# Retention attention and a top-1 expert layer on one core: states by chunks, one-hot placement, gathered rows

## The chip, the core and the metric

The program runs on one NeuronCore of a Trainium2 chip. Its engines have an instruction queue each: TensorE (PE in the rows; its weight loads are PEld), VectorE (DVE), ScalarE (ACT), GpSimd (POOL) and the queue that only issues transfers (SP). Matrix products are written to PSUM and are copied from there to SBUF by DVE or ACT; GpSimd does not read PSUM. The metric is device microseconds of one execution of the whole program, lower is better.

## The reference

Inputs are q, k and v of 8 batches, 8 heads, 576 positions and 64 channels, and the weights of 8 experts (512 to 1024 to 512), all float32.

```python
scores = q @ k.T / 8                               # per batch and head
gamma  = 1 - 2.0 ** (-5 - h)                       # per head
ret    = scores * where(i >= j, gamma ** (i - j), 0)
x      = (ret @ v), heads side by side             # 4608 tokens x 512
logits = x @ w_gate                                # 8 experts
e      = argmax(logits); gate = softmax(logits)[e] # one expert for a token
out    = gate * (relu(x @ w1[e]) @ w2[e])
```

There is no softmax in the attention. Because gamma ** (i - j) is gamma ** i times gamma ** -j, the decay can be multiplied into q and k beforehand, and only the triangular mask is left.

## The kernel before

**Attention, L156 to L268.** The loops go over 8 batches and 4 pairs of heads. SP loads both heads' q, k and v (L168, and L172 for the last 64 positions), and DVE multiplies the decay into q and k (L177 to L187). TensorE turns both with products against the identity (L197, L199, L208, L210); the two heads go to the lower and the upper 64 partitions of one PSUM tile, and DVE and ACT copy it out in turn (L203, L205, L212). For each of five blocks of k, TensorE multiplies it with all q at or after it (L225, L229); DVE masks the square on the diagonal (L231), and ACT copies what is right of it (L234, L236). All of these pass through one pool of four PSUM tiles, `psW`. Then the products with v are accumulated over the five blocks (L255, L259), and ACT copies the result, turned (channels by tokens), to `xTc` (L263 to L267). All of it is float32. A float32 product is two matmul instructions for TensorE, and so is each of these in the counts of the profile: 512 columns by 64 in L255 occur 64 times for 32 pairs of heads and head A.

**Routing, L269 to L347, once a batch.** The logits are computed turned (L272, L278). For each of five blocks of tokens they are turned back (L285), and so is x (L289, with the transpose instruction), which ACT casts to bfloat16 (L292). DVE finds the expert, the gate and, with two products against a triangle and a square of ones (L310, L312) and a running `carry`, the token's row in a table of 8 times 768 rows. GpSimd scatters the row of x (L332) and the token's number and gate (L340) into two DRAM tables, `sorted_x` and `sorted_meta`, which were filled with blanks at the start (L136, L143).

**Experts, L349 to L417.** For each expert ACT issues the loads of the weights (L362, L366; 2 MB each); ACT casts w1 (L364) and DVE w2 (L368). SP loads the expert's 768 rows turned, in two transfers of 384 (L380). For each 384 columns: 8 times 4 matmuls into `psh` (L392), ACT's relu to `hT` (L394), and for each of three blocks of 128 tokens 8 matmuls into `psy` (L399). DVE casts the token's number (L404) and multiplies by the gate (L406), and GpSimd scatters 128 rows of 2 KB to `out` (L408): 48 scatters in all. The framework sees every scatter as a write to all of `out`, so each one waits until the one before has landed; GpSimd works its queue in order. The order of the instructions in each queue is made by a list scheduler from their dependences and a cost model, with the order of the program as priority.

## Time and profile before

| | |
|---|---|
| median of three runs | 818.26 us |
| the runs | 823.42, 818.26, 817.86 us |
| span of the profiled execution | 826.1 us |
| mean granted TensorE clock of the profiled execution | 0.863 of full speed |
| DMA, mean over the span | 109 GB/s, 89.66 MB in all |
| DVE, ACT and POOL, busy share | 36%, 38%, 16% |

The profiled execution is 1.0% above the median of the runs. A busy time is the union of an engine's instructions; a matmul's end is modelled and includes the time its last column needs to come out, so that a busy TensorE is not one at its peak. In the granted clock 1.0 is 2.4 GHz and 0.5 is 1.2 GHz.

### The profile page before, as it was taken

The numbers are of one execution on the slowest core, as the hardware profiler recorded it, in microseconds if no ns is written. First come the engines' busy times: TensorE is split into PE (matmuls) and PEld (weight loads), VectorE is DVE, ScalarE is ACT, GpSimd is POOL, SyncE is SP. The second block draws the span as 40 slices with busy tenths as digits, with TensorE's granted clock in tenths as the row PEclk, the third lists the DMA queues.
The fourth block names the chain that finished last, engine by engine and source line by source line (L and its number), as shares of the span: only waits on it lengthen the run. The fifth ranks groups of instructions, "written<-read, shape, count | busy, mean of one in ns | idle before, by whom it ended". The sixth has DMA issues, their size and how long they took to land. (4 is left out here: it accounts for less than half of the span.)

```text
span 826.1 us, 13290 instructions
## 1 busy us (share of the span) xinstructions
PE 677.2 (82%) x4568; PEld 412.3 (50%) x4584; DVE 297.3 (36%) x1472; ACT 316.3 (38%) x889; POOL 134.1 (16%) x141
## 2 busy tenths in 40 slices
PE   0899899799999989989989989940967678599782
PEld 0666565565655656656556556530533243254341
DVE  4354444534534434534534453322121212212321
ACT  3244354344344335335325434412433144254230
POOL 0000400300310220120030040012011312213222
PEclk9999599789789789979959978965878797899997
DMA  9532232223223133223213222085798475553221
GB/s 301 129 80 58 58 80 67 56 68 80 55 54 80 30 74 78 51 60 80 58 52 87 59 59 58 18 302 156 247 348 246 158 182 166 180 152 89 59 68 58
DMA packets 175220, 89.66 MB, mean 109 GB/s; under 512 B 153262, under 2 KB 159406, under 8 KB 175152
## 3 DMA queue, kind: packets, MB, share of 16 engines
q1 hardware_dynamic: 155568, 41.04, 22.5%
q10 hardware_dynamic: 12544, 33.56, 11.6%
q0 software_dynamic: 7040, 14.21, 4.7%
q8 instruction: 36, 0.59, 0.4%
q14 instruction: 32, 0.26, 0.1%
HBM read 61.93 MB, written 24.21 MB: 104 GB/s over the span
## 5 line engine op out<-in xcount | busy, mean ns | idle before, releaser
L225 PE MATMUL psa<-qTp,kTp 64*128 64x512 f32 (+4 forms) x640 | 168.9, 485 | 22.6 <-ACT rt L234 19.0
L225 PEld LDWEIGHTS psa<-qTp,kTp 64*128 64x128 f32 (+1 forms) x640 | 87.9, 185 | 75.5 <-ACT rt L234 53.3
L399 PE MATMUL psy<-w2b,hT 128*128 128x512 bf16 x368 | 97.3, 411 | 32.9 <-DVE ysb L406 31.4
L392 PE MATMUL psh<-xTg,w1b 128*128 128x384 bf16 x512 | 95.9, 348 | 31.5 <-ACT w1b L364 18.2
L394 ACT ACTIVATE hT<-psh 128x384 bf16<-128x384 f32 x128 | 61.6, 490 | 143.3 <-PE psh L392 106.3
L332 POOL DMA_INDIRECT sorted_x<-xb,posi x40 | 39.3, 982 | 453.9 <-DVE mx L296 232.5
L234 ACT COPY rt<-psa 128x384 f32<-128x384 f32 (+3 forms) x256 | 88.3, 361 | 58.2 <-DVE rt L231 54.0
L255 PE MATMUL psxmB<-rt,tf 128*64 128x512 f32 (+3 forms) x256 | 105.6, 514 | 0.0
L255 PE MATMUL psxmA<-rt,tf 128*64 128x512 f32 (+3 forms) x256 | 104.9, 510 | 0.0
L199 PE MATMUL pst<-ident,tf 128*64 128x128 f32 x512 | 85.1, 316 | 17.4 <-DVE tf L177 17.4
L231 DVE TENSOR_TENSOR rt<-psa,trimask 128x128 f32<-128x128 f32 (+1 forms) x320 | 79.1, 268 | 43.8 <-PE psa L225 40.7
L197 PE MATMUL pst<-ident,tf 128*64 128x128 f32 x512 | 85.0, 316 | 11.3 <-ACT qTp L205 5.2
L392 PEld LDWEIGHTS <-w1b 128*128 128x128 bf16 x512 | 52.7, 103 | 74.0 <-issue 24.4
L408 POOL DMA_INDIRECT out_dram<-ysb,tid x48 | 54.0, 1124 | 198.6 <-DVE tid L404 96.7
L399 PEld LDWEIGHTS <-hT 128*128 128x128 bf16 x384 | 39.9, 104 | 85.2 <-issue 49.0
L197 PEld LDWEIGHTS pst<-ident,tf 128*64 128x64 f32 x512 | 64.4, 157 | 20.4 <-ACT qTp L205 11.0
L199 PEld LDWEIGHTS pst<-ident,tf 128*64 128x64 f32 x512 | 64.4, 157 | 17.8 <-DVE tf L177 17.8
L404 DVE CAST tid<-meta 128x1 int32<-128x1 f32 x48 | 7.4, 153 | 173.0 <-DMA out_dram<-ysb,tid 140.8
L259 PEld LDWEIGHTS psxqA<-rt,tf 128*64 128x64 f32 x256 | 38.4, 154 | 37.3 <-issue 28.5
L263 ACT COPY xTc<-psxmA 64x512 f32<-64x512 f32 x32 | 18.5, 578 | 97.4 <-PE psxmA L255 49.1
L203 DVE COPY qTp<-pst 128x128 f32<-128x128 f32 x64 | 18.6, 291 | 81.1 <-PE pst L199 61.9
L292 ACT CAST xb<-psx 128x512 bf16<-128x512 f32 (+1 forms) x40 | 23.4, 584 | 59.9 <-PE psx L289 43.4
(97 smaller groups left out, 927.4 us busy)
## 6 DMA issues: line engine op xcount, KB each, us to landing
w1f<-in_moe_w_dram ACTq DMA_DIRECT2D x8, 2048.0 KB, 8.1
w2f<-in_moe_w_dram ACTq DMA_DIRECT2D x8, 2048.0 KB, 9.5
tf<-in_q_dram SPq DMA_DIRECT2D x64, 128.0 KB, 2.4
tf<-in_k_dram SPq DMA_DIRECT2D x64, 128.0 KB, 2.4
tf<-in_v_dram SPq DMA_DIRECT2D x64, 128.0 KB, 2.4
sorted_x<-zin SPq DMA_DIRECT2D x1, 6144.0 KB, 20.3
tt<-in_q_dram SPq DMA_DIRECT2D x64, 16.0 KB, 2.2
tt<-in_k_dram SPq DMA_DIRECT2D x64, 16.0 KB, 2.2
```

What stands on the lines that cost most here:

```text
L197: nc.tensor.matmul(out=pst[0:Dh, 0:P], lhsT=tfA[:, c, :], rhs=ident[:, :], start=True, stop=True)
L199: nc.tensor.matmul(out=pst[Dh:2 * Dh, 0:P], lhsT=tfB[:, c, :], rhs=ident[:, :], start=True, stop=True)
L225: nc.tensor.matmul(out=psa[0:ni, 0:nA], lhsT=kTp[half:half + 64, c0:c0 + ni], rhs=qTp[half:half + 64, c0:c0 + nA], start=True, stop=True)
L231: nc.vector.tensor_tensor(out=rt[0:ni, 0:ni], in0=psa[0:ni, 0:ni], in1=trimask[0:ni, 0:ni], op=ALU.mult)
L234: nc.scalar.copy(out=rt[0:ni, ni:nA], in_=psa[0:ni, ni:nA])
L255: nc.tensor.matmul(out=psm[half:half + 64, c0:SM], lhsT=lhsV, rhs=rt[0:ni, 0:SM - c0], start=(i == 0), stop=last_main)
L259: nc.tensor.matmul(out=psq_[half:half + 64, 0:SQ], lhsT=lhsV, rhs=rt[0:ni, SM - c0:S - c0], start=(i == 0), stop=(i == nqb - 1))
L332: nc.gpsimd.indirect_dma_start(out=sorted_x[:, :], out_offset=bass.IndirectOffsetOnAxis(ap=posi[:, 0:1], axis=0), in_=xb16[:, :], in_offse ...
L392: nc.tensor.matmul(out=psh[0:P, 0:GT], lhsT=w1b[:, c, fb * P:(fb + 1) * P], rhs=xTg[:, c, :], start=(c == 0), stop=(c == NDC - 1))
L394: nc.scalar.activation(out=hT[:, fb, :], in_=psh[0:P, 0:GT], func=AF.Relu)
L399: nc.tensor.matmul(out=psy[0:P, 0:Dm], lhsT=hT[:, fc, blk * P:(blk + 1) * P], rhs=w2b[:, fc, :], start=(fc == 0), stop=(fc == NFB - 1))
L408: nc.gpsimd.indirect_dma_start(out=out[:, :], out_offset=bass.IndirectOffsetOnAxis(ap=tid[:, 0:1], axis=0), in_=ysb[:, :], in_offset=None, ...
```

## The change

The kernel is written anew; the shapes are constants.

- **Attention by chunks.** The work goes in 40 units, 5 for a batch: 4 pairs of heads over 512 positions in 4 chunks of 128, and one unit for the last 64 positions of all 8 heads. GpSimd multiplies the decay into k and q (`kk`, `qq`, in `stage_T`), and TensorE turns them with the transpose instruction. A state for each pair of heads, k times v summed over the chunks up to each, is accumulated in PSUM (`stage_S`) and copied by ACT into block-diagonal tiles `sall`. Scores are computed within a chunk only (`stage_SC`); one DVE instruction per head masks all four chunks. `stage_AV` adds scores times v and, for the chunks after the first, q times the state of the chunks before. `stage_XR` multiplies the result with a matrix that is the identity beside the gate's weights, so that x by rows and the pair's share of the logits come out of one product; ACT casts x to bfloat16, and SP stores it to `x_rows` in DRAM, in token order.
- **Order.** Every TensorE instruction is pinned to program order: scores of unit i, rows of unit i - 1, transposes and state of unit i + 1, then the values of unit i. Each PSUM tile has a name and one buffer of its own.
- **Routing in two halves** of 2304 tokens, 20 columns of 128: after batch 3 (during units of batches 4 and 5), and at the end of the attention. The expert, the gate and the token's rank are found for all 20 columns at once; `place` builds one-hot matrices of slots (`rh`, 128 by 128 per column) and a payload per column, and 20 (then 40) matmuls put the tokens' numbers and gates into the slots of all experts.
- **Experts in two passes**: 256 slots per expert from the first half and 384 for the rest, 5 blocks of 128 per expert and 40 in all. A block's rows are fetched from `x_rows` by an indirect gather (`gather`, GpSimd) and turned by TensorE (`trans`). Weights come in pieces of 512 KB on SP's queue; those of two experts are loaded during the attention and cast by GpSimd, the others four pieces a step with casts in turn on ACT, DVE and GpSimd. The scatter to `out` is as before, with the slots' numbers made beforehand and four buffers.
- **A general path** behind a branch at the end runs all tokens that found no slot, if an expert's second pass would need more than 384.
- The blank-filled tables, their zeroing, the transposing loads and the scatters of x and of the numbers are gone.

The added code, cut to its core (the removed code stands above):

```diff
+NT = B * NCOL
+GT = NT // 2
+CA = 256
+CB = 384
...
+    def pin(i):
+        tc.keep_in_program_order(i)
+        return i
+    def mm(out, lhsT, rhs, start, stop):
+        return pin(nc.tensor.matmul(out=out, lhsT=lhsT, rhs=rhs, start=start, stop=stop,
+                                    skip_group_check=True))
...
+        def kv(dst, src, hs):
+            if hs is None:
+                for c in range(NCH):
+                    nc.sync.dma_start(out=dst[:, c, :, :],
+                                      in_=src[b, :, c * P:(c + 1) * P, :].rearrange("h p d -> p h d"))
+            else:
+                for h in range(hs.start, hs.stop):
+                    nc.sync.dma_start(out=dst[:, :, h, :],
+                                      in_=src[b, h, 0:NCH * P, :].rearrange("(c p) d -> p c d", p=P))
...
+    loads = {0: load_batch(0, 4)}
...
+    casts = [nc.gpsimd.tensor_copy, nc.scalar.copy, nc.vector.tensor_copy]
+    def load_w(e, part, eng):
...
+        st = stpool.tile([P, F], F32, tag="st", name="wst")
+        c = part % 4
+        if part < 4:
+            nc.sync.dma_start(out=st[:, :], in_=moe_w1[e, c * P:(c + 1) * P, :])
+            casts[eng](out=w1b[:, c, :, :, :].rearrange("p j s m -> p j m s"),
+                       in_=st[:, :].rearrange("p (j m s) -> p j m s", m=P, s=2))
...
+    def stage_T(u):
+        b, p = u
+        qt, kt, vt, qk, vr = loads[b]
+        if p < NP:
+            h0 = 2 * p
+            kk = wkp.tile([P, NCH, P], F32, tag="kk")
+            nc.gpsimd.tensor_tensor(
+                out=kk[:, :, :].rearrange("p c (h d) -> p c h d", d=DH), in0=kt[:, :, h0:h0 + 2, :],
+                in1=kg[:, 0:NCH, h0:h0 + 2].unsqueeze(3).to_broadcast([P, NCH, 2, DH]), op=ALU.mult)
+            qq = wkp.tile([P, NCH, P], F32, tag="qq")
...
+            psq = ps1.tile([P, 4 * P], F32, tag="Q")
+            for s in range(4):
+                pin(nc.tensor.transpose(out=psq[:, s:4 * P:4], in_=qq[:, s, :], identity=ident[:, :]))
+            psk = ps1.tile([P, 4 * P], F32, tag="K")
+            for c in range(NCH):
+                pin(nc.tensor.transpose(out=psk[:, c * P:(c + 1) * P], in_=kk[:, c, :], identity=ident[:, :]))
+            qT = wkp.tile([P, 4 * P], F32, tag="qT")
+            nc.vector.tensor_copy(out=qT[:, :], in_=psq[:, :])
+            kT = wkp.tile([P, 4 * P], F32, tag="kT")
+            nc.scalar.copy(out=kT[:, :], in_=psk[:, :])
+            st_[u] = dict(kk=kk, qT=qT, kT=kT)
...
+        pss = ps1.tile([P, NCH, DH], F32, tag="S")
+        for c in range(NCH):
+            n = NCH - c
+            for j in range(2):
+                mm(pss[j * DH:(j + 1) * DH, c:NCH, :], kk[:, c, j * DH:(j + 1) * DH],
+                   vt[:, c, 2 * p + j, :].unsqueeze(1).to_broadcast([P, n, DH]), c == 0, c == NCH - 1)
+        sa = sall[b % 2]
+        nc.scalar.copy(out=sa[0:DH, p, :, 0:DH], in_=pss[0:DH, :, :])
+        nc.scalar.copy(out=sa[DH:P, p, :, DH:P], in_=pss[DH:P, :, :])
...
+            for c in range(NCH):
+                for ps, r in ((psa, slice(0, DH)), (psb, slice(DH, P))):
+                    mm(ps[:, c, :], kT[r, c * P:(c + 1) * P], qT[r, c * P:(c + 1) * P], True, True)
...
+            nc.vector.tensor_tensor(out=sa[:, :, :], in0=psa[:, :, :], in1=m, op=ALU.mult)
+            nc.vector.tensor_tensor(out=sb[:, :, :], in0=psb[:, :, :], in1=m, op=ALU.mult)
...
+            psx = ps1.tile([P, NCH, P], F32, tag="XT")
+            for c in range(NCH):
+                for j in range(2):
+                    mm(psx[j * DH:(j + 1) * DH, c, :], vt[:, c, 2 * p + j, :], d["sc"][j][:, c, :], c == 0, False)
+            for c in range(1, NCH):
+                mm(psx[:, c, :], sl[:, p, c - 1, :], qT[:, c * P:(c + 1) * P], False, c == NCH - 1)
+            xT = wkp.tile([P, NCH, P], F32, tag="xT")
+            nc.scalar.copy(out=xT[:, :, :], in_=psx[:, :, :])
...
+        psr = ps1.tile([P, 2, 512], F32, tag="XR")
+        n = P if p < NP else REM
+        for c in range(4):
+            mm(psr[0:n, c // 2, (c % 2) * IWN:(c % 2 + 1) * IWN], xT[:, c, :],
+               iw[:, p if p < NP else c, :], True, True)
...
+            nc.scalar.copy(out=xr[:, 0:NCH, p * P:(p + 1) * P].rearrange("p (a c) f -> p a c f", c=2),
+                           in_=r[:, :, :, 0:P])
+                nc.vector.tensor_tensor(out=l, in0=r[:, :, :, P:IWN], in1=l, op=ALU.add)
+                nc.sync.dma_start(out=x_rows[b * S:b * S + NCH * P, :].rearrange("(c p) d -> p c d", p=P),
+                                  in_=xr[:, 0:NCH, :])
...
+        mm(psr[:, 0:n], su1[:, :], oh[:, g, :, :].rearrange("p e t -> p (e t)"), True, False)
+        mm(psr[:, n:n + E], onesb[:, :], incl[:, :, GT - 1], False, False)
+        mm(psr[:, 0:n], onesb[:, :], incl[:, :, :].rearrange("p e t -> p (e t)"), False, True)
...
+    def place(ph, pool, psp):
+        nb = (CA if ph == 0 else CB) // P
+        nt = GT if ph == 0 else NT
+        w = E * nb
...
+        for f in range(NFLD):
+            eng = nc.vector if f % 2 == 0 else nc.gpsimd
+            eng.tensor_tensor(out=pay[:, :, f, :], in0=ohb[:, :, :, :].rearrange("p t b e -> p t (b e)"),
+                              in1=fld[:, 0:nt, f].unsqueeze(2).to_broadcast([P, nt, w]), op=ALU.mult)
+        rh = pool.tile([P, nt, P], BF16, tag=f"rh{ph}")
+        for t in range(nt):
+            nc.vector.tensor_scalar(out=rh[:, t, :], in0=iota_r[:, :], scalar1=r[:, t:t + 1], scalar2=None,
+                                    op0=ALU.is_equal)
+        for t in range(nt):
+            mm(psp[:, 0:NFLD * w], rh[:, t, :], pay[:, t, :, :].rearrange("p f w -> p (f w)"), t == 0, t == nt - 1)
...
+    def gather(e, ph):
+        nb = (CA if ph == 0 else CB) // P
+        nr = NTOK // 2 if ph == 0 else NTOK
+        for j in range(nb):
+            i = j * E + e
+            xg = gp.tile([P, DM], BF16, tag="xg", name="xg")
             nc.gpsimd.indirect_dma_start(
+                out=xg[:, :], out_offset=None, in_=x_rows[0:nr, :],
+                in_offset=bass.IndirectOffsetOnAxis(ap=slots[ph][1][:, i:i + 1], axis=0),
+                bounds_check=nr - 1, oob_is_err=False)
+            gat_t[(e, ph, j)] = xg
...
+    stage_T(units[0])
+    stage_S(units[0])
+    for i, u in enumerate(units):
+        b, p = u
+        if p == 0 and b + 1 < B:
+            loads[b + 1] = load_batch(b + 1, 1)
+        stage_SC(u)
+        if i > 0:
+            stage_XR(units[i - 1])
+        if i + 1 < len(units):
+            stage_T(units[i + 1])
+        if i + 1 < len(units):
+            stage_S(units[i + 1])
+        stage_AV(u)
+        for (e, pt) in w_at.get(i, []):
+            load_w(e, pt, 0)
+        if u == (B // 2, 1):
+            incl0 = softmax_top1(0, rtmp)
+        if u == (B // 2, 2):
+            ps = ps1.tile([P, 512], F32, tag="Q")
+            ranks(0, incl0, rtmp, ps)
+        if u == (B // 2 + 1, 0):
+            ps = ps1.tile([P, 512], F32, tag="Q")
+            place(0, rtmp, ps)
+        if u == (B - 2, 0):
+            gather(0, 0)
+            gather(1, 0)
+    stage_XR(units[-1])
...
+    seq = [(0, 0), (1, 0), (0, 1), (1, 1)] + [(e, ph) for e in range(2, E) for ph in (0, 1)]
...
+            for c in range(NPT):
+                pin(nc.tensor.transpose(out=pt[:, c, :], in_=xg[:, c * P:(c + 1) * P], identity=identb[:, :]))
+            nc.vector.tensor_copy(out=xt[:, :, j * P:(j + 1) * P], in_=pt[:, :, :])
...
+        per = 2 if ph == 0 else 1
+        for f0 in range(0, NFB, per):
+            pm = psH.tile([P, per, n], F32, tag="ph")
+            for o in range(per):
+                fb = f0 + o
+                for c in range(NPT):
+                    mm(pm[:, o, :], w1b[:, c, fb // 2, fb % 2, :], xt[:, c, :], c == 0, c == NPT - 1)
+            nc.scalar.activation(out=ht[:, f0:f0 + per, :], in_=pm[:, :, :], func=AF.Relu)
...
+            py = psY.tile([P, DM], F32, tag="py")
             for fb in range(NFB):
+                mm(py[:, :], ht[:, fb, j * P:(j + 1) * P], w2b[:, fb // 2, fb % 2, :], fb == 0, fb == NFB - 1)
+            ys = yp.tile([P, DM], F32, tag="ys")
+            nc.vector.tensor_scalar(out=ys[:, :], in0=py[:, :], scalar1=gat[:, i:i + 1], scalar2=None, op0=ALU.mult)
+            nc.gpsimd.indirect_dma_start(
+                out=out[:, :], out_offset=bass.IndirectOffsetOnAxis(ap=tids[:, i:i + 1], axis=0),
+                in_=ys[:, :], in_offset=None, bounds_check=NTOK - 1, oob_is_err=False)
...
+            load_w(e, pt, (1, 2, 0)[nq[0] % 3])
...
+    trans(0, 0)
+    more_w(4)
+    incl1 = softmax_top1(1, rtm2)
+    for i, (e, ph) in enumerate(seq):
+        ht = mm1(e, ph)
+        if i == 0:
+            ps = psT.tile([P, 512], F32, tag="pt", name="psrk")
+            ranks(1, incl1, rtm2, ps)
+        if i + 1 < len(seq):
+            trans(*seq[i + 1])
+        mm2(e, ph, ht)
+        if i == 0:
+            ps = psT.tile([P, 512], F32, tag="pt", name="pspl")
+            place(1, rtm2, ps)
+        if i + 2 < len(seq):
+            gather(*seq[i + 2])
+        more_w(4)
...
+    over = nc.values_load(fi[0:1, 0:1], min_val=0, max_val=NTOK,
+                          skip_runtime_bounds_check_because="a count of tokens")
+    with tc.If(over > 0):
...
```

## Rows read from the trace of the kernel before

**Rows 1.** The page: busy times; granted clock in tenths, in 40 slices.

```profile
PE 677.2 (82%) x4568; PEld 412.3 (50%) x4584; DVE 297.3 (36%) x1472; ACT 316.3 (38%) x889; POOL 134.1 (16%) x141
...
PEclk9999599789789789979959978965878797899997
```

**Rows 2.** Stretches: start:end, length, busy time by engine, clock, DMA share.

```profile
...
0.00:22.00 22.00, 1.94 (x8) 1.56 (x8) 8.31 (x61) 7.93 (x33) 1.75 (x13) 1.00 0.93 299
22.00:546.00 524.00, 485.51 (x3672) 316.89 (x3672) 228.20 (x1275) 217.11 (x716) 70.64 (x72) 0.88 0.28 69
546.00:592.00 46.00, 16.20 (x73) 8.41 (x74) 9.31 (x39) 12.79 (x15) 7.90 (x9) 0.60 0.66 213
592.00:746.00 154.00, 116.94 (x535) 57.03 (x544) 31.78 (x61) 55.33 (x84) 31.48 (x28) 0.84 0.69 206
746.00:826.00 80.00, 56.63 (x284) 28.45 (x287) 19.75 (x38) 23.10 (x41) 22.36 (x20) 0.91 0.24 67
```

**Rows 3.** The chain that ended last: shares, then pieces (start, us).

```profile
DMA out_dram<-ysb,tid 17%; POOLq L408 0%; POOLq L442 0%
...
643.94 2.68 DMA out_dram<-ysb,tid
656.14 5.80 DMA out_dram<-ysb,tid
```

**Rows 4.** The scatters to `out`; GpSimd's last two (start, us).

```profile
L408 POOL DMA_INDIRECT out_dram<-ysb,tid x48: 966/971/2468, 591.9 to 822.2; - x48
...
818.84 0.97 POOL L408 DMA_INDIRECT out_dram<-ysb,tid  x1 [2.48 <-DMA out_dram<-ysb,tid]
822.18 0.97 POOL L408 DMA_INDIRECT out_dram<-ysb,tid  x1 [2.37 <-DMA out_dram<-ysb,tid]
```

**Rows 5.** TensorE in order of time, one head pair (start, us).

```profile
306.79 1.53 PE L225 MATMUL psa<-qTp,kTp 64*128 64x512 f32 x4
...
311.14 1.41 PE L225 MATMUL psa<-qTp,kTp 64*128 64x192 f32 x8 [0.78 <-ACT rt L234]
312.48 0.64 PE L255 MATMUL psxmA<-rt,tf 128*64 128x512 f32 x1
312.49 0.64 PE L255 MATMUL psxmB<-rt,tf 128*64 128x512 f32 x1
312.96 0.59 PE L255 MATMUL psxmA<-rt,tf 128*64 128x512 f32 x1
313.39 0.22 PE L259 MATMUL psxqA<-rt,tf 128*64 128x64 f32 x1
...
315.56 0.32 PE L197 MATMUL pst<-ident,tf 128*64 128x128 f32 x1
```

**Rows 6.** TensorE, the turning of x (four transposes merged).

```profile
538.49 0.65 PE L289 MATMUL psx<-ident,xTc 128*128 128x128 f32 x4
```

**Rows 7.** Groups by line and shape: count, busy us, mean ns, idle.

```profile
L406 DVE TENSOR_SCALAR ysb<-psy,meta 128x512 f32<-128x512 f32 x48 | 34.0, 745 | 11.4 <-PE psy L399 11.4
L292 ACT CAST xb<-psx 128x512 bf16<-128x512 f32 x32 | 18.7, 585 | 52.5 <-PE psx L289 43.4 <-DMA sorted_x<-xb,posi 9.1
L234 ACT COPY rt<-psa 128x320 f32<-128x320 f32 x64 | 26.7, 425 | 20.6 <-DVE rt L231 19.0
L231 DVE TENSOR_TENSOR rt<-psa,trimask 128x128 f32<-128x128 f32 x256 | 69.4, 283 | 42.5 <-PE psa L225 39.3
L177 DVE TENSOR_TENSOR tf<-tf,gq 128x256 f32<-128x256 f32 x64 | 26.8, 419 | 16.1 <-DMA tf<-in_q_dram 16.0
L332 POOL DMA_INDIRECT sorted_x<-xb,posi x40 | 39.3, 982 | 453.9 <-DVE mx L296 232.5 <-DVE carry L324 79.2 <-DVE mtx L315 46.4
```

**Rows 8.** GpSimd at the start: start, length, instruction.

```profile
1.13 0.28 POOL masks.py:199 TENSOR_SCALAR_AFFINE_SELECT ident<-ident 128x128 f32<-128x128 f32 x1
```

**Rows 9.** TensorE in the experts' stage: eight matmuls of 512 columns, and the next.

```profile
758.65 1.89 PE L399 MATMUL psy<-w2b,hT 128*128 128x512 bf16 x8 [0.39 <-DVE ysb L406]
760.37 0.33 PE L392 MATMUL psh<-xTg,w1b 128*128 128x384 bf16 x1
```

More of the change, by code (lines that the diff above doesn't have):

```diff
@@ L17 @@
 I32 = mybir.dt.int32
+PSUM = bass.MemoryType.PSUM
 P = 128
[L20 to L24 removed]
+B, H, S, DH = 8, 8, 576, 64
+DM = H * DH
+E, F = 8, 1024
+NP = H // 2
+NCH = 4
+REM = S - NCH * P
+NCOL = NCH + 1
+NT = B * NCOL
+GT = NT // 2
+NFB = F // P
+NPT = DM // P
+IWN = P + E
+CA = 256
+CB = 384
+NTOK = B * S
+NFLD = 5
 @with_exitstack
@@ new lines @@
+    tri = attc.tile([P, P], F32, name="tri")
+    make_upper_triangular(nc, tri[:, :], val=1.0, diag=True)
+    iw = attc.tile([P, NP, IWN], F32, name="iw")
+    nc.sync.dma_start(out=iw[:, :, P:IWN], in_=moe_w_gate.rearrange("(c p) e -> p c e", p=P))
+    for p in range(NP):
+        nc.gpsimd.tensor_copy(out=iw[:, p, 0:P], in_=ident[:, :])
+    lns = []
+    for h in range(H):
+        L = float(np.log1p(-(2.0 ** (-5.0 - h))))
+        L1 = float(round(L * 4096.0) / 4096.0)
+        lns.append((L1, L - L1))
@@ new lines @@
+    nc.vector.tensor_copy(out=kg[0:REM, NCH, :], in_=qg[0:REM, NCH, :])
+    sall = []
+    for j in range(2):
+        t = attc.tile([P, NP, NCH, P], F32, name=f"sall{j}")
+        nc.gpsimd.memset(t[:, :, :, :], 0.0)
+        sall.append(t)
+    lg = rt.tile([P, NT, E], F32, name="lg")
+    nc.gpsimd.memset(lg[:, :, :], 0.0)
+    su1 = consts.tile([P, P], BF16, name="su1")
+    nc.gpsimd.memset(su1[:, :], -1.0)
+    nc.gpsimd.affine_select(out=su1[:, :], in_=su1[:, :], pattern=[[-1, P]], base=0, channel_multiplier=1,
+                            compare_op=ALU.is_ge, fill=0.0)
@@ new lines, with more_w @@
+    wq = [(e, i) for e in range(2, E) for i in range(8)]
+    nq = [0]
+    def more_w(n):
+        while n > 0 and nq[0] < len(wq):
+            e, pt = wq[nq[0]]
+            load_w(e, pt, (1, 2, 0)[nq[0] % 3])
+            nq[0] += 1
+            n -= 1
+    trans(0, 0)
[15 more added lines that the diff above has]
+        more_w(4)
```

720 lines of the change are left out of this document (368 added, 352 removed).

## The prediction

> **What bounds the kernel now.** I read the stretches first. From 22 to 546 us, the attention with its routing, TensorE is busy for 485.5 of 524 us, and DVE (228.2), ACT (217.1), GpSimd (70.6) and the transfers (share 0.28) are far from it [rows 2]. But that busy time is not work at TensorE's rate. In order of time, the products with v run at a steady pace: the second instruction on 512 columns starts at 312.96 and its successor at 313.39, 0.43 us, and the other head's starts 0.01 us after the first one's, in the other half of the array. A float32 product is two such instructions, so a column costs 1.68 ns for both heads at once. The whole stretch from 312.48 to 315.56 has 1,600 columns (512 + 384 + 256 + 128 and five times 64): 1.93 ns each. The scores before it, from 306.79 to 312.48, also have 1,600 (512 + 448 + 320 + 192 + 64, and 64) and take 3.56 ns each; TensorE waits there for copies out of four shared PSUM tiles, 0.78 us once for ACT [rows 5]. From 546 to 592 us nearly everything stands: TensorE is busy for 16.2 of 46 us, at a mean granted clock of 0.60 [rows 2].
>
> The experts' stage is bounded by something else. The chain that ended last is one scatter to `out` after the other [rows 3]: 48 of them from 591.9 to 822.2 us. The last two start 3.34 us apart, 0.97 of it issue and 2.37 waiting for the one before [rows 4]. While weights are loaded 28 scatters take 154 us, 5.5 each, and afterwards 20 take 80 us, 4.0 each [rows 2]; a landing is 2.68 us where nothing disturbs and 5.80 elsewhere [rows 3].
>
> **The change, part by part.**
>
> *Products of the attention.* For a pair of heads the new order has these columns at the paired rate: states 256 + 192 + 128 + 64 = 640, scores 4 x 128 = 512, values 512 and states' share 3 x 128 = 384, rows and logits 4 x 136 = 544; in sum 2,592 in place of 3,200 and the routing's turned logits. I take 1.93 ns, the rate of the stretch whose form most of them have (64 or 128 columns of weights, halves of the array in turn): 5.0 us. The bounds are 1.68 and 3.56 ns. Eight transposes at 0.65 / 4 = 0.16 us [rows 6] add 1.3: 6.3 us. The unit of the last 64 positions has 256 + 512 + 544 = 1,312 columns and four transposes: 3.2 us. A batch is 4 x 6.3 + 3.2 = 28.4, and eight are 227 us. For the changes between its five stages I add 0.4 us a unit (an estimate, as the 0.39 us wait in [rows 9]), 16 us: **243 us** in place of 524.
>
> *What must hide beside 6.7 us a unit.* DVE: one copy and two masks of 512 columns at 0.745 (the 128-column mask's 0.283 is the lower end) and a small addition, 2.4 us. ACT: three copies of 512 at 0.585 and two of 256 at 0.43, 2.6 us [rows 7]. They lie on TensorE's path only by latency: the order puts two stages between every product and the reader of its copy, so the shared PSUM pool's wait should go; what is late next is a copy queued behind another on the same engine. GpSimd: no product of two inputs runs there before; its nearest row is a 128-column select of 0.28 us [rows 8], so 512 columns cost at most four times that, 1.1, and at least DVE's 0.84 (twice the 0.419 for 256 [rows 7]). Two products and half a weight cast (1,024 columns, 2.2 us by the same row, every second unit) make 3.3 us. The Trainium skill's GPSIMD Engine Reference (4.1, Engine selection) speaks against this placement: an elementwise operation on a tile belongs on VectorE, as GpSimd is about two times slower with two inputs. By that rule a product is an estimated 1.7 us and GpSimd's part of a unit 4.5: the sum stays, but the distance to TensorE's 6.7 falls from 3.4 to 2.2 us. No run here shows such a product yet. Transfers: 28.3 MB of q, k and v, 4.7 of rows stored and 8.4 of early weights, 41.4 MB in 243 us, 170 GB/s; 69 GB/s took a share of 0.28 [rows 2], so 170 takes 0.69. That cover is the thinnest.
>
> *Routing.* The per-batch chain of L269 to L347 leaves TensorE's path, with its products, its copies and the half clock after it [rows 1]. In its place TensorE, pinned, waits for two chains on DVE. For the first half: 20 one-hot tiles at 0.28 (the 128-column mask as the upper end), three payloads at about 0.5 and a dozen small instructions at 0.2 make **10 us**, uncovered. At the end it is 40 tiles and wider payloads, some 20 us, of which the first step of an expert covers 8: **12 us**, in place of the 46 us before the first scatter [rows 2].
>
> *Start.* In the first 22 us TensorE works for 1.94 [rows 2], as the loads of the second head stand behind the zeroing of the tables on SP's queue. That goes. GpSimd has some 25 small instructions (0.28 each) and a product before the first transpose: **9 us**, between 5 and 22.
>
> *Experts.* A block's eight matmuls of 512 take 1.72 us [rows 9], 0.42 ns a column. An expert has 20,480 columns in each of its two layers and 20 transposes (0.16 at most): 18.9 us, 151 for eight. The scatters are 40 in place of 48 and still each wait for the last. The least is 40 x 3.34 = 134 us. With 30 while weights are loaded and ten after, the old intervals give 30 x 5.5 + 10 x 4.0 = 205. I take 4.6 for the thirty, between 3.34 and 5.5, since the transposing loads and the cast of the numbers between two scatters go, while the weights stay: 138 + 40 = **178 us**, more than TensorE's 151. Five gathers an expert (0.98 us of issue, as L332 [rows 7]) and 2.7 casts on GpSimd have to fit into the scatters' waits of 2.4 us.
>
> *End.* 822.2 to 826.1 is 3.9 us; with a read of the count and a branch I take **6**. The branch itself isn't taken: the reference's arithmetic on its own inputs puts at most 353 tokens of an expert into the second pass, and 384 fit.
>
> Sum: 9 + 243 + 10 + 12 + 178 + 6 = 458 us against the span of 826.1. The profiled execution is 1.0% above the median of 818.26, so the forecast is 458 x 818.26 / 826.1 = **454 us**. With the ends of rates and chains it goes from 420 to 505.
>
> **The rivals.**
>
> 1. *Both stages at their floor, 380 us.* At 1.68 ns and with stage changes hidden the attention is 204 us, and if every scatter takes near 3.4 us TensorE's 151 binds: 9 + 204 + 5 + 8 + 151 + 6 = 383 of span. For it: four times fewer, larger copies. Against it: two engines at over 0.9 of their rate at once. Chance 0.14.
>
> 2. *TensorE goes on waiting as in the scores, 589 us.* Every PSUM tile has one buffer, so a late copy stops a pinned queue. At 3.56 ns the attention is 379 us and the span 594. For it: that rate is what four shared buffers gave [rows 5]. Against it: no wait is left between neighbouring stages. Chance 0.11.
>
> 3. *GpSimd's queue adds up in the experts' stage, 528 us.* If gathers and casts fall between scatters and not into their waits, an expert takes 5 x 4.6 + 5 x 0.98 + 2.7 x 2.2 = 33.8 us while weights are cast, and 25 afterwards: 253 in place of 178. For it: the queue is worked in order and each scatter's wait stops it. Against it: the gathers are ready long before the scatter. Chance 0.13.
>
> 4. *GpSimd's products set the pace; the slower side.* There are 72 of them, and 16 casts (35 us). They bind from 2.8 us a product on; the kernel is slower than before if 72 products take 611 - 35 us, from 8 us each on. For it: two products a unit are the largest work that this engine gets, and DVE reads beside it. Against it: the rows' 0.84 to 1.1. At four times DVE's 0.84, 3.4 us, the attention is 280 us and the kernel 490. Chance of binding 0.04, of ending above 826 half of that.
>
> **How the numbers follow.** The forecast has 0.58, the rivals 0.14, 0.11, 0.13 and 0.04. The range goes from 385 to 560: it holds the forecast's own range, rival 3, and half of rival 1, whose 380 is an end at which both stages must be perfect, and leaves out rival 2 and the slower half of rival 4, about 0.2. The bound of 1% is what a measurement of this kernel can tell from no change (its runs differ by 0.7%). Faster by over 1% are all cases but the worst of rival 4, and a queue order that nobody intended: 0.96; within 1% 0.01; slower 0.03.
>
> **What would show it.** Right: the last unit's rows before 290 us; a pair's unit of 6 to 7 us with TensorE busy for most of it and the clock at 1.0 except around the two placements; 40 scatters in some 180 us, each waiting for the one before; GpSimd's products near 1 us. Wrong: waits of a unit's scores for `qT`, `kT`, or of the values for the masks, over 0.5 us (rival 2); gathers or casts between two scatters with the matmuls standing (rival 3); GpSimd busy through the attention (rival 4); loads of the next batch landing after its first product, which would break the cover of 0.69. The sum is most sensitive to the 1.93 ns: a tenth of it is 20 us.

## The result, and the profile after

The changed kernel takes 520.7 us (median of four, 518.0 to 525.1) against 820.8 us for the kernel before: a ratio of 0.639, interval 0.632 to 0.645. The ratio goes by the fast runs alone, and one of the four runs before, 834.3 us, was slow; the quotient of the two medians, 0.634, lies inside the interval. The forecast was 454 us, with 420 to 505 as the ends of its own rates, and the range 385 to 560. The profiled execution took 518.0 us, its span is 516.2.

The page of the changed kernel, busy times and granted clock, the lines that answer to [rows 1]:

```profile
PE 407.9 (79%) x3714; PEld 303.6 (59%) x3714; DVE 197.2 (38%) x398; ACT 186.9 (36%) x300; POOL 277.0 (54%) x237
...
PEclk9999999999998999899995968869789596899985
```

Its stretches, columns as in [rows 2] (the last number is GB/s): the attention up to the first placement, from there to the last row, up to the first scatter, the second placement, the scatters while weights arrive, the rest.

```profile
12.00:167.00 155.00, 149.76 (x1703) 129.45 (x1701) 66.03 (x149) 57.34 (x118) 83.00 (x61) 0.99 0.87 198
167.00:256.00 89.00, 84.68 (x978) 73.20 (x978) 32.46 (x67) 42.96 (x70) 46.40 (x33) 0.98 0.55 173
256.00:266.00 10.00, 8.48 (x67) 5.70 (x66) 8.97 (x36) 2.72 (x5) 0.00 (x0) 1.00 0.04 10
266.00:309.00 43.00, 27.13 (x153) 15.87 (x154) 21.73 (x63) 11.50 (x13) 28.37 (x18) 0.74 0.22 70
309.00:447.00 138.00, 90.31 (x516) 51.35 (x514) 48.22 (x55) 54.21 (x60) 86.30 (x54) 0.81 0.52 187
447.00:504.00 57.00, 47.27 (x303) 27.71 (x300) 14.11 (x24) 16.54 (x32) 21.19 (x22) 0.95 0.21 77
```

Up to 256 us TensorE is busy for 234 of 244 us at a clock near 1.0. From 266 to 447 us it is busy for 117 of 181, at 0.74 and 0.81. The attention became what was forecast; the experts' stage did not.

The scatters to `out`, by their line (count, shortest, median and longest ns, first and last start); this and the last two in time, below it, answer to [rows 4]:

```profile
L584 POOL DMA_INDIRECT out_dram<-ys,tids x40: 971/998/1886, 266.2 to 503.5; - x40
```

```profile
500.03 0.97 POOL L584 DMA_INDIRECT out_dram<-ys,tids  x1 [2.53 <-DMA out_dram<-ys,tids]
503.51 0.97 POOL L584 DMA_INDIRECT out_dram<-ys,tids  x1 [2.51 <-DMA out_dram<-ys,tids]
```

Forty scatters take 237 us where 178 were forecast. The 25th starts at 446.8 us, so the first 24 intervals average 7.5 us and the last 15 average 3.8. What fills the former is seen on GpSimd and on ScalarE in order of time (start, length, instruction, idle time before it and its releaser):

```profile
299.53 1.00 POOL L584 DMA_INDIRECT out_dram<-ys,tids  x1 [2.59 <-issue]
302.58 12.29 POOL L211 CAST w1b<-wst 128x1024 bf16<-128x1024 f32 x2 [2.05 <-PE pm L59]
...
319.27 1.02 POOL L584 DMA_INDIRECT out_dram<-ys,tids  x1 [0.30 <-issue]
```

```profile
318.23 1.04 ACT L216 CAST w2b<-wst 128x1024 bf16<-128x1024 f32 x1 [3.16 <-DMA wst<-in_moe_w_dram]
319.18 1.87 ACT L570 ACTIVATE ht<-pm 128x384 bf16<-128x384 f32 x4
...
330.77 4.89 ACT L211 CAST w1b<-wst 128x1024 bf16<-128x1024 f32 x1 [7.42 <-DMA wst<-in_moe_w_dram]
338.99 1.04 ACT L216 CAST w2b<-wst 128x1024 bf16<-128x1024 f32 x1 [3.33 <-DMA wst<-in_moe_w_dram]
339.94 1.56 ACT L570 ACTIVATE ht<-pm 128x512 bf16<-128x512 f32 x3
```

TensorE in the same stretch:

```profile
319.71 3.11 PE L59 MATMUL pm<-xt,w1b 128*128 128x384 bf16 x12 [3.24 <-ACT ht L570]
...
328.95 2.78 PE L59 MATMUL pm<-xt,w1b 128*128 128x256 bf16 x24
340.58 1.86 PE L59 MATMUL pm<-xt,w1b 128*128 128x256 bf16 x8 [8.84 <-ACT ht L570]
```

From 323 to 340 us ScalarE waits 7.4 us for a load, casts for 4.9, waits 3.3 for the next load and casts again; only then come the three relus (`ht`) for which TensorE's finished products wait, and TensorE stands for 8.84 us. Over the whole run its longest-lasting waits are these (us in total, times, longest):

```profile
PE pm L59 <- ACT ht L570: 28.3, 6, 12.7
PE pt L553 <- DVE xt L554: 21.2, 4, 10.4
PE psq L237 <- POOL qq L231: 11.7, 1, 11.7
PE pspl L59 <- DVE rh L461: 8.6, 1, 8.6
```

The first two are relus and evictions behind casts; the third is the start, the fourth the second placement. The load queue waits in turn for buffers that casts release (SyncE's own waits, 257 to 450 us):

```profile
SPq L214 <- DVE xt L554: 65.8, 4, 49.4
SPq L214 <- POOL w1b L211: 47.7, 6, 12.6
SPq L210 <- POOL w2b L216: 39.9, 5, 10.8
```

Its longest stand, 49.4 us up to 305.6 us, is put down to `xt`, which no load reads. It ends with four w1 casts that start at 302.55 to 302.58 us on ScalarE, VectorE and GpSimd, each released by a product of TensorE (`pm`): four pieces fill the four staging buffers until expert 0 gives back one of the three sets of weights.

What a cast costs stands in the groups by shape (count, busy us, mean ns, idle before); L227 and L231 are the new products on GpSimd, L289 one of VectorE's masks:

```profile
L211 POOL CAST w1b<-wst 128x1024 bf16<-128x1024 f32 x16 | 80.0, 5066 | 6.9 <-PE psb L59 2.7 <-DMA wst<-in_moe_w_dram 2.1 <-PE pm L59 2.1
L211 ACT CAST w1b<-wst 128x1024 bf16<-128x1024 f32 x8 | 39.2, 4962 | 8.2 <-DMA wst<-in_moe_w_dram 7.4 <-PE pm L59 0.8
L231 POOL TENSOR_TENSOR qq<-qt,qg 128x512 f32<-128x512 f32 x32 | 34.8, 1092 | 52.2 <-PE psq L237 37.9 <-PE psq L252 8.6 <-issue 4.7
L227 POOL TENSOR_TENSOR kk<-kt,kg 128x512 f32<-128x512 f32 x32 | 33.8, 1056 | 12.8 <-PE pss L59 11.8 <-DMA vt<-in_v_dram 0.6 <-POOL kq L248 0.4
L211 DVE CAST w1b<-wst 128x1024 bf16<-128x1024 f32 x8 | 25.9, 3233 | 38.0 <-PE pm L59 25.3 <-DMA wst<-in_moe_w_dram 8.1 <-ACT ht L570 4.6
L289 DVE TENSOR_TENSOR sa<-psa,tri 128x512 f32<-128x512 f32 x32 | 22.4, 700 | 97.8 <-PE psb L59 96.9 <-PE psa L59 0.9
...
L216 POOL CAST w2b<-wst 128x1024 bf16<-128x1024 f32 x16 | 17.0, 1074 | 0.8 <-DMA wst<-in_moe_w_dram 0.8
L216 ACT CAST w2b<-wst 128x1024 bf16<-128x1024 f32 x8 | 8.4, 1045 | 47.7 <-DMA wst<-in_moe_w_dram 42.8 <-PE py L59 4.9
L216 DVE CAST w2b<-wst 128x1024 bf16<-128x1024 f32 x8 | 8.3, 1038 | 34.5 <-DMA wst<-in_moe_w_dram 34.5
```

A cast of 1,024 columns takes 1.04 to 1.07 us for w2, which keeps its order, and 5.07, 4.96 and 3.23 us for w1, whose columns L211 puts down in another order.

### The profile page after: what moved, and what is told of

The parts are those of the page before. It is cut to its first block, busy times and chain, and to the rows that moved or that the text cites. A ratio compares the mean times of both kernels' runs of the same rounds, so it can differ in the third digit from the quotient of the medians.

```text
span 516.2 us, 9296 instructions
## 1 busy us (share of the span) xinstructions
PE 407.9 (79%) x3714; PEld 303.6 (59%) x3714; DVE 197.2 (38%) x398; ACT 186.9 (36%) x300; POOL 277.0 (54%) x237
## 5 line engine op out<-in xcount | busy, mean ns | idle before, releaser
L59 PE MATMUL pm<-xt,w1b 128*128 128x256 bf16 (+1 forms) x512 | 79.7, 315 | 31.2 <-ACT ht L570 28.3
L584 POOL DMA_INDIRECT out_dram<-ys,tids x40 | 41.3, 1031 | 113.9 <-DVE ohb L448 29.2
L570 ACT ACTIVATE ht<-pm 128x384 bf16<-128x384 f32 (+1 forms) x96 | 50.0, 535 | 93.3 <-PE pm L59 91.4
L211 POOL CAST w1b<-wst 128x1024 bf16<-128x1024 f32 x16 | 80.0, 5066 | 6.9 <-PE psb L59 2.7
L59 PE MATMUL py<-w2b,ht 128*128 128x512 bf16 x320 | 79.4, 406 | 2.0 <-ACT ht L570 2.0
L231 POOL TENSOR_TENSOR qq<-qt,qg 128x512 f32<-128x512 f32 x32 | 34.8, 1092 | 52.2 <-PE psq L237 37.9
L488 POOL DMA_INDIRECT xg<-x_rows,tidg x40 | 50.3, 1257 | 17.9 <-DVE gat L476 8.4
L289 DVE TENSOR_TENSOR sa<-psa,tri 128x512 f32<-128x512 f32 x32 | 22.4, 700 | 97.8 <-PE psb L59 96.9
L59 PE MATMUL psr<-iw,xT 128*128 128x136 f32 (+1 forms) x320 | 48.3, 295 | 4.3 <-ACT xT L316 3.0
L59 PE MATMUL psa<-qT,kT 64*128 64x128 f32 (+1 forms) x320 | 43.4, 277 | 3.6 <-DVE qT L242 3.6
L59 PE MATMUL pss<-vt,kk 128*64 128x128 f32 (+3 forms) x512 | 44.0, 317 | 0.0
L59 PE MATMUL psb<-qT,kT 64*128 64x128 f32 (+1 forms) x320 | 43.5, 277 | 0.0
L211 ACT CAST w1b<-wst 128x1024 bf16<-128x1024 f32 x8 | 39.2, 4962 | 8.2 <-DMA wst<-in_moe_w_dram 7.4
L227 POOL TENSOR_TENSOR kk<-kt,kg 128x512 f32<-128x512 f32 x32 | 33.8, 1056 | 12.8 <-PE pss L59 11.8
L211 DVE CAST w1b<-wst 128x1024 bf16<-128x1024 f32 x8 | 25.9, 3233 | 38.0 <-PE pm L59 25.3
```

Of the source, the lines that this page charges most:

```text
L59: return pin(nc.tensor.matmul(out=out, lhsT=lhsT, rhs=rhs, start=start, stop=stop, skip_group_check=True))
L211: casts[eng](out=w1b[:, c, :, :, :].rearrange("p j s m -> p j m s"), in_=st[:, :].rearrange("p (j m s) -> p j m s", m=P, s=2))
L227: nc.gpsimd.tensor_tensor(out=kk[:, :, :].rearrange("p c (h d) -> p c h d", d=DH), in0=kt[:, :, h0:h0 + 2, :], in1=kg[:, 0:NCH, h0:h0 + 2] ...
L231: nc.gpsimd.tensor_tensor(out=qq[:, :, :].rearrange("p s (h d) -> p h s d", d=DH), in0=qt[:, h0:h0 + 2, :, :], in1=qg[:, 0:NCH, h0:h0 + 2] ...
L289: nc.vector.tensor_tensor(out=sa[:, :, :], in0=psa[:, :, :], in1=m, op=ALU.mult)
L488: nc.gpsimd.indirect_dma_start(out=xg[:, :], out_offset=None, in_=x_rows[0:nr, :], in_offset=bass.IndirectOffsetOnAxis(ap=slots[ph][1][:, ...
```

## The experiments

My theory after the two traces: the w1 casts are three to five times too long (A), and the loads behind them wait for staging buffers (B). The rival was GpSimd's order, with eleven gathers between two scatters (C). Ratios are against the kernel before on the same chip; the last columns are starts of the first, 12th and last scatter in the profiled run.

| run | us | ratio, interval | scatter 1 | 12 | 40 |
|---|---|---|---|---|---|
| the change | 520.7 | 0.639 (0.632 to 0.645) | 266.2 | 360.8 | 503.5 |
| a_plain_w1 | 487.5 | 0.594 (0.590 to 0.599) | 257.2 | 339.0 | 473.6 |
| b_stage8 | 509.2 | 0.621 (0.616 to 0.626) | 266.9 | 360.9 | 498.3 |
| c_no_more_weights | 451.7 (one run) | | 261.7 | 328.6 | 435.4 |
| d_products_on_DVE | 515.3 | 0.633 (0.627 to 0.638) | 267.0 | 351.9 | 496.7 |
| e_rows_twice | 566.7 | 0.695 (0.690 to 0.699) | 314.9 | 408.4 | 552.9 |
| f_placement_later | 516.3 | 0.633 (0.629 to 0.637) | 266.6 | 357.7 | 503.5 |
| g_room_for_weights | 471.8 | 0.579 (0.575 to 0.583) | 256.5 | 345.3 | 456.9 |
| h_room_and_placement_later | 470.2 | 0.577 (0.573 to 0.580) | 258.1 | 344.9 | 456.3 |
| i_casts_a_step_later | 466.0 | 0.568 (0.564 to 0.571) | 257.4 | 344.4 | 452.6 |
| j_casts_and_placement_later | 465.6 | 0.568 (0.564 to 0.572) | 257.2 | 342.9 | 451.4 |
| k_loads_without_casts | 457.3 | 0.556 (0.554 to 0.558) | 257.7 | 333.2 | 441.5 |
| l_casts_without_loads | 454.3 | 0.554 (0.553 to 0.555) | 261.9 | 331.5 | 439.3 |

**a_plain_w1.** The w1 cast keeps the order of the columns; the rows of w2 are loaded to match.

```diff
-            casts[eng](out=w1b[:, c, :, :, :].rearrange("p j s m -> p j m s"),
-                       in_=st[:, :].rearrange("p (j m s) -> p j m s", m=P, s=2))
+            casts[eng](out=w1b[:, c, :, :, :].rearrange("p j s m -> p (j s m)"), in_=st[:, :])
...
-    in_=moe_w2[e, ...].rearrange("(p s) d -> p s d", s=2)
+    in_=moe_w2[e, ...].rearrange("(s p) d -> p s d", s=2)
```

> w1's pieces are cast without the re-ordering of their columns (and w2's rows are loaded in the matching order, in runs of 2 KB in place of 4). The changed kernel's casts of w1 took 5.07 us on GpSimd, 4.96 on ACT and 3.23 on DVE, those of w2 1.07, 1.05 and 1.04. Theory A, the experts' stage is late because of these casts, which stop relu, copies and scatters behind them and hold the staging buffers: each of the five groups of four w1 pieces after 302 us gets 4 to 8 us shorter, 20 to 40 us in all, 480 to 500 us. Theory B, the four staging buffers and the weights' transfer set the pace whatever the cast costs: 512 us or more. Theory C, the order on GpSimd's queue (gathers between scatters): 16 casts there get 4 us shorter, but scatters stay 6 us apart while weights are loaded, 505 to 515.

487.5 us, as A expected. The same groups by shape in this run:

```profile
L211 POOL CAST w1b<-wst 128x1024 bf16<-128x1024 f32 x16 | 16.6, 1045 | 4.2 <-DMA wst<-in_moe_w_dram 4.2
L211 ACT CAST w1b<-wst 128x1024 bf16<-128x1024 f32 x8 | 8.3, 1043 | 7.6 <-DMA wst<-in_moe_w_dram 7.4 <-PE pm L59 0.2
L211 DVE CAST w1b<-wst 128x1024 bf16<-128x1024 f32 x8 | 6.7, 836 | 33.0 <-PE pm L59 27.4 <-DMA wst<-in_moe_w_dram 5.6
```

Of the 30 us of span some 9 come off before the first scatter. About half of them were casts of expert 2 that stood in the attention. In the changed kernel, ScalarE there:

```profile
204.13 4.76 ACT L211 CAST w1b<-wst 128x1024 bf16<-128x1024 f32 x1
208.40 0.70 ACT L273 COPY sall<-pss 64x256 f32<-64x256 f32 x1
209.11 0.37 ACT L274 COPY sall<-pss 64x256 f32<-64x256 f32 x1
209.50 0.58 ACT L316 COPY xT<-psx 128x512 f32<-128x512 f32 x1
209.98 4.76 ACT L211 CAST w1b<-wst 128x1024 bf16<-128x1024 f32 x1
```

From one cast of x to the next (`xr`), the unit around them took 11.6 us, and 6.8 in a_plain_w1; on TensorE the rows of this unit and the next took 16.4 and 12.1 us. The other half lies at the first placement: one of VectorE's one-hot tiles, begun at 157.7 us, was done only at 163.1, when a w1 cast on GpSimd (from 157.62, 4.72 us) and the product behind it had ended, and TensorE waited 3.6 us for the copy of q queued behind the tiles. In a_plain_w1 that cast takes 1.03 us. The other 21 us are between the first scatter and the last.

**b_stage8.** Experts 3 to 7 are staged in eight buffers of their own.

```diff
-        st = stpool.tile([P, F], F32, tag="st", name="wst")
+        st = (stpool if e < 3 else st2[0]).tile([P, F], F32, tag="st", name="wst")
...
+    st2.append(p2.enter_context(tc.tile_pool(name="wstage2", bufs=8)))
```

> Eight staging buffers of their own for the pieces of experts 3 to 7, casts as in the changed kernel. Theory A (casts): no change within 1.5%, as the casts keep their length on the three queues. Theory B (staging): the next four pieces land while the last four are cast, the period of an expert's weights falls from 33 towards 20 us, 480 to 495 us. Theory C (GpSimd's order): no change.

509.2 us lies between A's answer and B's. Staging buffers alone are worth some 2%: the casts still hold their engines, and the load queue still stands 37.2 us in one piece, until the casts of expert 3 begin (ScalarE's at 297.6 us).

**c_no_more_weights.**

```diff
-    wq = [(e, i) for e in range(2, E) for i in range(8)]
+    wq = []
+    for e in range(2, E):
+        wb[e] = wb[e % 2]
```

> Leaves out the loads and casts of experts 2 to 7; their blocks are computed with the weights of experts 0 and 1. What remains is the placement of the second half, gathers, products and scatters. A and B (the weights' path is the whole excess): after the placement the scatters follow at 3.4 to 3.8 us, as in the last 57 us of the changed kernel, 430 to 445 us. C: the gathers between them keep the distance near 5, above 470.

451.7 us in one run, a little over what A and B gave and far below C's bound. All gathers are there, eleven of them between the second scatter (269.9 us) and the third (291.4), and yet the 37 scatters from 295.0 us on come 3.9 us apart. TensorE paces them (columns as above):

```profile
309.00:369.00 60.00, 59.12 (x402) 36.69 (x401) 17.82 (x31) 20.15 (x38) 29.96 (x30) 1.00 0.27 90
```

An expert takes it 18.9 us, 3.8 for each of five scatters. C falls: the later gathers cost nothing. What the first eleven cost, this run doesn't tell, as it keeps them: behind the second placement, for which TensorE stands 8.6 us, it waits another 2.1 us for gathered rows. Some 70 us belong to the weights of experts 2 to 7.

**d_products_on_DVE.** The three products of `stage_T` (L227, L231, L248) run on VectorE.

```diff
-            nc.gpsimd.tensor_tensor(
+            nc.vector.tensor_tensor(
...
```

> The decay is multiplied into q and k by VectorE in place of GpSimd, nothing else. If TensorE's columns set the pace of the attention (the prediction's step, 6.07 us a unit), DVE's 2.4 us a unit rise to about 4.1 and still hide: within 1.5% of the changed kernel, 513 to 528. If GpSimd's products (1.06 and 1.09 us) paced the units, faster by 2% or more. If one-buffer latency is the limit, the longer queue on DVE delays the masks and the copy of q: a unit of 6.5 us or more, 535 and up.

515.3 us, within 1.5%; the intervals overlap, and the last rows leave at 256.1 us against 255.1. GpSimd's products cost nothing where they are.

**e_rows_twice.**

```diff
         for c in range(4):
-            mm(psr[...], xT[:, c, :], iw[...], True, True)
+            for _ in range(2):
+                mm(psr[...], xT[:, c, :], iw[...], True, True)
```

> Every matmul that makes the attention's rows (four of 136 columns a unit, eight passes that follow each other at 0.116 us in the trace) is issued twice with the same result, so TensorE gets 8 x 0.116 = 0.93 us more in each of the 40 units and nothing else changes. If TensorE's instructions pace the attention, as the prediction's 243 us have it: units 7.0 us apart in place of 6.07, the first scatter some 37 us later (near 303 us), and the run at 548 to 560 us. Rival: the attention's loads pace it (their DMA share is 0.85 there), or VectorE and ScalarE do: units stay within 0.2 us of 6.07 and the run below 530 us.

Undisturbed units come 7.00 us apart in place of 6.07, to the hundredth what TensorE's added instructions make. The time is 567 us, over the expected range, because four units between 150 and 199 us (from one cast of x to the next on ScalarE) took 20.1, 8.1, 8.6 and 12.5 us. There ScalarE's queue holds an early cast of expert 2 that waits for its load:

```profile
160.36 4.70 ACT L211 CAST w1b<-wst 128x1024 bf16<-128x1024 f32 x1 [6.50 <-DMA wst<-in_moe_w_dram]
165.09 0.59 ACT L316 COPY xT<-psx 128x512 f32<-128x512 f32 x1
```

and TensorE waits for that `xT` (its waits: us in total, times, longest):

```profile
PE psr L59 <- ACT xT L316: 10.8, 1, 10.8
```

This one wait is nearly the 12 us by which the first scatter comes later than the expected 303. The attention is paced by TensorE, and a cast in the wrong queue stops it.

**f_placement_later.**

```diff
-        if i + 1 < len(seq):
+        if i == 1:
+            ps = psT.tile([P, 512], F32, tag="pt", name="pspl")
+            place(1, rtm2, ps)
+            gather(*seq[2])
+        if i + 1 < len(seq) and i != 1:
             trans(*seq[i + 1])
         mm2(e, ph, ht)
-        if i == 0:
-            ps = psT.tile([P, 512], F32, tag="pt", name="pspl")
-            place(1, rtm2, ps)
-        if i + 2 < len(seq):
+        if i == 1:
+            trans(*seq[2])
+        if i > 0 and i + 2 < len(seq):
```

> The changed kernel with one move: the second placement's matmuls stand behind expert 1's first matmul block in place of ahead of it, and the transposes of the rows of expert 0's second pass stand behind expert 1's second block. That covers the 8.6 us in which TensorE waits for the one-hot tiles. If weights pace the stage that follows (long casts, four staging buffers, three sets of weights), the time is given back there: 512 to 521 us, within 1.5% of the changed kernel. Rival: the placement's gap lies on the path by itself: 8 to 12 us come off, 508 to 512 us.

516.3 us, within 1.5%, intervals overlapping. The third scatter came at 287.2 us in place of 295.9, the fifth at 317.0 in place of 319.3: given back to the weights.

**g_room_for_weights** and **h_room_and_placement_later** (the same with f's move).

```diff
+            wp = st2[1] if e in (3, 4) else wpool
...
-        st = stpool.tile([P, F], F32, tag="st", name="wst")
+        st = (st2[0] if late[0] else stpool).tile([P, F], F32, tag="st", name="wst")
...
+    for n_ in range(8):
+        w_at.setdefault(len(units) - 8 + n_, []).append((2, n_))
-    wq = [(e, i) for e in range(2, E) for i in range(8)]
+    wq = [(e, i) for e in range(3, E) for i in range(8)]
...
+    st2.append(p2.enter_context(tc.tile_pool(name="wstage2", bufs=4)))
+    st2.append(p2.enter_context(tc.tile_pool(name="wts2", bufs=2)))
```

> a_plain_w1 (w1 cast in plain order) with room added: expert 2's weights are loaded in the last 8 units of the attention, experts 3 and 4 have two sets of weight buffers of their own in the experts' stage, and that stage has four staging buffers beside the four of the attention. The same bytes are moved and the same number of casts runs. If release of buffers is what was left of the loss after plain casts (487.5 us there, 451.7 us with no weights to load after expert 1): 453 to 466 us, scatters 3.5 to 4.2 us apart after the second placement, TensorE's clock near 1.0. Rival: the transfer itself is the limit (25 MB for six experts at the 200 to 230 GB/s of the stage, 110 to 125 us, or contention with the scatters' and gathers' rows): 475 to 488 us.

> g_room_for_weights with the move of f_placement_later. If TensorE's order paces the stage once weights no longer do, the 8.6 us of waiting for one-hot tiles and part of the gathers behind it now count: 7 to 14 us below g_room_for_weights, 442 to 456 us. Rival: the wait only moves (TensorE stands as long for the gathers of expert 0's second pass behind expert 1's blocks), or the chain of 40 scatters sets the end (40 x 3.5 us from the first scatter is only 140 us of some 175, so it should not): within 4 us of g_room_for_weights.

471.8 us misses both ranges, and 470.2 is no measurable difference from it. Room took 16 us off a_plain_w1; the load queue's longest stand after 250 us fell from 41.6 to 8.0 us. Which part of the room did it (the early loads, the sets of weights, the staging buffers), these runs don't tell. What was left sat between the first scatter and the 12th, 89 us against 67 in c_no_more_weights; from the 12th to the last the two take 112 and 107.

**i_casts_a_step_later** and **j_casts_and_placement_later** (with f's move).

```diff
+        if late[0]:
+            pend.append(cast)
...
     def more_w(n):
+        todo = pend[:]
+        del pend[:]
+        for cast in todo:
+            cast()
...
+    st2.append(p2.enter_context(tc.tile_pool(name="wstage2", bufs=8)))
```

> g_room_for_weights with each late cast issued one step (some 9 us) after its load, and eight more staging buffers in place of four. In g_room_for_weights the scatters between 297 and 365 us still came 6 to 7 us apart, with ScalarE's casts waiting 35 us in all for their transfers and VectorE's 16 us, and relus and evictions behind them in the same in-order queues. If that queueing is what is left: 455 to 464 us, scatters 3.5 to 4.5 us apart from 300 us on. Rival: the burst of transfers itself slows the stage (243 to 288 GB/s between 250 and 310 us), or the weights land too late: 468 to 476 us.

> i_casts_a_step_later with the second placement moved behind expert 1's first matmul block (the move of f_placement_later, which was worth 0 to 4 us twice while weights paced the stage). If the casts no longer wait, the placement's standing of TensorE (8 to 10 us, and part of the gathers behind it) shows: 5 to 12 us below i_casts_a_step_later, 445 to 457 us. Rival: TensorE stands as long for the gathers of expert 0's second pass: within 3 us.

Both also have eight late staging buffers in place of four, so the gain over g_room_for_weights is of the two together. 466.0 and 465.6 us, again short of the expected gain. The waits behind casts did go; of TensorE's in i_casts_a_step_later the largest after the start, and what is left of the two that led before:

```profile
PE pspl L59 <- POOL pay L464: 10.8, 1, 10.8
PE pt L563 <- DVE xt L564: 8.6, 7, 2.8
...
PE pm L59 <- ACT ht L580: 1.3, 1, 1.3
```

28.3 us became 1.3, and 21.2 became 8.6. Yet the first 12 scatters still take 87 us. j_casts_and_placement_later ties with it and stands 55 us below the change; it is the fastest of the kernels that compute everything.

**k_loads_without_casts** and **l_casts_without_loads.**

```diff
+        if e >= 3:
+            wb[e] = wb[e % 3]
...
-            pend.append(cast)
+            pass
```

In the second the casts read one tile of a constant, and the two load instructions become conditional:

```diff
-            nc.sync.dma_start(out=st[:, :], in_=moe_w1[...])
+            if not late[0]:
+                nc.sync.dma_start(out=st[:, :], in_=moe_w1[...])
```

> i_casts_a_step_later with the casts of experts 3 to 7 left out (their loads land in the staging buffers and are not used; the experts compute with the weights of experts 0 to 2). In i_casts_a_step_later the first 12 scatters take 87 us, in c_no_more_weights 67 us, the other 28 scatters 108 and 107 us. If the transfers' bytes cost those 20 us (gathers, scatters and evictions beside 240 to 380 GB/s): 460 to 467 us, within 1% of i_casts_a_step_later. If the casts' places in the engines' queues do: 443 to 455 us.

> i_casts_a_step_later with the loads of experts 3 to 7 left out (their casts run, from one tile of a constant, into the same weight buffers). If the transfers cost the 20 us: 443 to 455 us. If the casts' places in the queues do, or their time on ScalarE and VectorE, as the relus and evictions stand behind them: 460 to 467 us.

Without casts 8.8 us go, without loads 11.8: the first 12 scatters take 75.5 and 69.6 us. k lies between its two answers, l fits the transfers'. Neither alone is the cause. The two gains add to more than the 14.3 us between i_casts_a_step_later and c_no_more_weights, as they would if a load and its cast are links of one chain. k is more than i without casts: as no cast holds a staging buffer, its loads run at 392 GB/s from 257 to 309 us, against 269 in i. Beside them its third to sixth scatters come 7.0 us apart, 4.1 in c_no_more_weights, and the longest landing of a scatter is 7.1 us, against 3.8 there and 3.6 in l. So the transfers do slow scatters beside them. Whether that is their cost in i, or when they land, these runs don't tell.

## Why the prediction was right and where it failed

The measured 520.7 us lies outside the forecast's own 420 to 505 us. That the stated range holds it is owed to the room left for rival 3, whose mechanism is only half borne out: that much is luck. The forecast of the span was 458 us, the span is 516.2. Term by term, from the profiled run:

| term | forecast | measured |
|---|---|---|
| start (first transpose at 11.7 us) | 9 | 11.7 |
| attention with the first placement (to the last row, 255.7 us) | 243 + 10 | 244.0 |
| from there to the first scatter | 12 | 10.5 |
| 40 scatters | 178 | 237.3 |
| end | 6 | 12.7 |

The rest of the 67 us between 454 and the median is the reduction by 1% to the median of before (4 us) and this profiled run's place (it is 2.7 us below its median, its span 1.8 below its own time).

**Attention: right, and for the reason given.** A pair's unit is 6.07 us for 6.7, the last unit 4.25 for 3.6, a batch 28.5 for 30.4 with the changes of stage. TensorE's passes in order of time, a whole group of rows and of transposes:

```profile
102.29 1.14 PE L59 MATMUL psr<-iw,xT 128*64 128x136 f32 x8
103.36 0.66 PE L237 MATMUL psq<-ident,qq 128*128 128x128 f32 x4
103.85 0.60 PE L240 MATMUL psk<-ident,kk 128*128 128x128 f32 x4
```

Eight passes of 136 columns start 0.116 us apart, 1.71 ns a column for the two passes of a product: near the lower bound of 1.68, where I had taken 1.93 [rows 5]. That is the rows alone: without the 1.02 us of its eight transposes (forecast 1.3) a unit takes 5.05 us for 2,592 columns, 1.95 ns with the changes of stage in it, for 5.4 us forecast. e_rows_twice shows by intervention that these instructions pace the stage, which rival 2 denied. The cover was thinner than I had it up to 167 us, a DMA share of 0.87 at 198 GB/s for the forecast 0.69 at 170; it held.

**GpSimd's products: right.** 1.06 and 1.09 us, inside 0.84 to 1.1; d_products_on_DVE excludes rival 4. The Trainium skill's GPSIMD Engine Reference (4.1, Engine selection) would have VectorE do them at half the time. Measured, the same products took a median of 0.68 and 0.69 us on VectorE in d_products_on_DVE, against 1.06 and 1.05 on GpSimd: the ratio is about 1.5, and here it decided nothing.

**Placements: smaller than forecast, and the second in another place.** At the first, given 10 us, TensorE's longest wait was the 3.6 us for the copy of q. At the second it stood 8.6 us for the one-hot tiles (forecast 12), but between the second scatter and the third: these are inside the 237.3 us, and the 10.5 us beside the 12 in the table are expert 0's first block. Moving that wait gained nothing in f, h or j.

**Experts: wrong, and the step that failed is the thirty scatters at 4.6 us.** The first thirty intervals averaged 6.8 us. The 4.6 took the weights for nearly free: "the cast of the numbers between two scatters go, while the weights stay". Three things were missed. A cast was priced at 2.2 us from a select of 128 columns [rows 8]; w1's took 5.07 us on GpSimd, and w2's 1.07. Only GpSimd's casts were counted at all, while two thirds of those of experts 2 to 7 run on ScalarE and VectorE, ahead of relus and evictions in queues that are worked in order. And no term stood for how weights come in, with four staging buffers and three sets of weights, each released by work further down those queues. The load queue's single stand of 49.4 us shows the last of the three at its worst. c_no_more_weights takes all three out: its 40 scatters need 173.7 us. That this is near the forecast's 178 is luck: there the scatters' chain was to set the pace, above TensorE's 151, and in c_no_more_weights TensorE sets it, as half of rival 1 had it. Its 18.9 us an expert are the prediction's own number, whose parts, 17.2 us of products and 20 transposes at 0.16, add up to 20.4. After the last load the scatters of the changed kernel come 3.8 us apart, for 4.0.

Rival 3, at 528 us, is nearest in time, but the mechanism is only half its own: casts did stand between scatters, gathers did not matter, and the longest stands of TensorE were for ScalarE and VectorE, not for GpSimd.

**End: 6.7 us short.** The last scatter's issue ends at 504.5 us, and 11.7 us of span follow in which no engine does counted work; before it was 2.9. No run tried to shorten it.

## What to carry to other kernels

Price every instruction that a change lets loose on an engine by its access pattern, not only by its size, and look at what stands behind it in that engine's queue: a cast that waits for its load holds up the relu behind it, and the matmuls behind the relu. When loads, casts and compute share queues, take the whole chain of a weight out once (load, cast, buffer); that one run sizes the problem before its links are tried one by one, and shows what paces the rest. A wait that is moved while something else paces the stage is given back.
